# Expert 0's input from one-hot products, three expert lists from one-hot rows, held weights, and a pool of their own for the last block's rows

## The chip, the cores and the metric

The kernel runs on one core of a Trainium2 chip. TensorE (PE) multiplies, VectorE (DVE) and ScalarE (ACT) do elementwise work, GpSimd (POOL) issues the indirect transfers, SyncE (SP) issues the plain ones. The metric is the device time of one execution in microseconds. A kernel is timed several times and the median is quoted.

## The reference

Three stages, all in fp32: attention within hash buckets, an MLP with silu, and a top-1 choice of 8 experts with a skip gate.

```python
def _moe_ref(x, w_in, w_out):                 # x 1536 x 512, w_in 512 x 2048
    h = x @ w_in
    g = h * (1.0 / (1.0 + np.exp(-h)))
    return (g @ w_out).astype(np.float32)
def _moe2_ref(x, w_skip, w_gate, w1, w2):     # w1 8 x 512 x 1024, w2 8 x 1024 x 512
    do_compute = x @ w_skip > 0
    out = x.copy()
    xc = x[do_compute]
    logits = xc @ w_gate
    e_idx = np.argmax(logits, axis=1)
...
    for e in range(E):
        mask = e_idx == e
        h = np.maximum(xc[mask] @ w1[e], 0.0)
        y[mask] = gate_w[mask, None] * (h @ w2[e])
    out[do_compute] = xc + y
```

`gate_w` is the softmax probability of the chosen expert. A token with a skip score of zero or less keeps its row x.

## The kernel before

The span has three parts. Attention runs to about 237 us. Then come the MLP items: three blocks of 512 tokens, 16 slices of the 2048 hidden columns each. An item is 12 hidden matmuls (`ph`, L608) and 12 output matmuls (`o`, L642 and L651), because every fp32 number is split into a high and a low part and three products are added. The last part routes the tokens and runs the eight experts.

Weights arrive in pieces of 512 KB (`wraw`, issued by `fill`). ScalarE casts the high part `whi` (L249), VectorE subtracts to get the low part `wlo` (L252). Each expert uses eight such pieces. There are only a few places ("homes") for split pieces; `ahead()` splits the next piece whenever a matmul group has given its home back.

Routing works by block. Logits of blocks 0 and 1 are made on VectorE beside the MLP items, four at a time (`logit`, L664). `route` then finds each token's expert, its rank among the tokens of that expert (matmuls with a triangle and with ones) and its slot in a list. For experts 0 and 1 a one-hot matrix `oh` (L745) times token numbers gives the list at once (L752, L767). All lists are also written to DRAM by four GpSimd scatters a block (`id_d`, L780).

The last block's route stands in the way of the experts. Its MLP output is transposed (`xt`, L946), its logits are made by matmul (`pl`, L949), turned (`plc`, L960) and routed; the rows go to `x_d` in DRAM. Expert 0's rows are then fetched by an indirect transfer through `eid` (`xg`, L672, `fetch_x`), transposed (`tr`, L1027) and split (`xTh` L1020, `xTl` L1021); only then its first matmul (`eh`, L1049) can run. `em_busy` (L973) issues matmuls whose result nobody reads, while TensorE has nothing else to do.

Lists of experts 2 to 7 are read back from DRAM (`eidr`, L1001), transposed and cast (L1126) after expert 1's first hidden product. Gate values go to DRAM (`g_d`) and are fetched by list (`ggc`, `fetch_g`). At an expert's end VectorE makes `eo` (L1079), gate times output plus row, and GpSimd scatters it (L1010).

What runs when is written by hand. `plan` is a list of steps: ("h", e, c, j) is a quarter of expert e's hidden products, ("y", e, j) a quarter of its output products, ("t", e, c) the transposes of a hidden half (`hT0`, `hT1`), ("x", e) the transposes of the fetched rows. Each engine runs its instructions in the order in which the program issues them.

Of the kernel before, what the change touches and what calls it, by code (L numbers as in the profile page):

```python
# [9 lines left out]
F32 = mybir.dt.float32  # L10
# [9 lines left out]
P = 128  # L20
BIG = 2.0 ** 40
NB = 6


@with_exitstack
def kernel(
# [68 lines left out]
    list1 = cp.tile([P, 1], F32, name="list1")  # L95
# [494 lines left out]
    ggc = sm.tile([P, NE, 2], F32, name="ggc", bufs=1)  # L590
# [79 lines left out]
    def gathered(ix, src, cols, tag, xg=None):  # L670
        xg = pools["e"].tile([P, cols], F32, tag=tag, name=tag, bufs=4) if xg is None else xg
        nc.gpsimd.indirect_dma_start(  # L672
            out=xg, out_offset=None, in_=src, in_offset=bass.IndirectOffsetOnAxis(ap=ix, axis=0),
            bounds_check=NTOK, oob_is_err=False)
        return xg
# [4 lines left out]
    def fetch_g(e):  # L680
        ggs[e] = gathered(eid[:, e:e + 1], g_d, 1, "gg", ggc[:, e, 0:1])


    def route(t0, t1, Lx, ps, idx, ps0=None):

        n = t1 - t0
        last = t1 == NT
        if t0 == 0:
            nc.tensor.matmul(idx, c_one, c_dum, start=True, stop=False)
        Lt, st, cm = Lx[:, :, 0:NE], sel[:, t0:t1], cmp_[:, t0:t1]  # L690
        pr = ps[:, 0:n * NE].rearrange("p (t e) -> p t e", e=NE)
        pr0 = ps0[:, 0:n].unsqueeze(2) if last else pr[:, :, 0:1]

        def base(pr, w):

            nc.tensor.matmul(pr, c_one, pre[:, t0, 0:w].unsqueeze(1).to_broadcast([P, n, w]), start=True, stop=False)

        def ranks(pr, st, w):

            for t in range(n - 1):  # L700
                nc.tensor.matmul(pr[:, t + 1:n], c_one, st[:, t:t + 1].to_broadcast([P, n - 1 - t, w]), start=False, stop=False)
            nc.tensor.matmul(pr, c_u, st, start=False, stop=True)

        if last:
            base(pr0, 1)
        base(pr, NE)
        mx = sm.tile([P, n], F32, tag="mx", name="rmx")
        nc.vector.tensor_reduce(mx, Lt, axis=AX.X, op=ALU.max)
        nc.vector.tensor_scalar(cm, Lx[:, :, NE], 0.0, None, op0=ALU.is_gt)
        eq = sm.tile([P, n, NE], F32, tag="eq", name="eq")  # L710
        em = c_em.unsqueeze(1).to_broadcast([P, n, NE])
        nc.vector.tensor_tensor(eq, Lt, mx.unsqueeze(2).to_broadcast([P, n, NE]), op=ALU.is_equal)
        if last:

            st0 = sm.tile([P, n, 1], BF16, name="st0", bufs=1)
            nc.vector.tensor_tensor(st0, eq[:, :, 0:1], cm.unsqueeze(2), op=ALU.mult)
            ranks(pr0, st0, 1)
            yield
        else:
            st0 = st[:, :, 0:1]  # L720

        def choice():
            nc.vector.tensor_tensor(eq, eq, em, op=ALU.mult)
            ix = sm.tile([P, n], F32, tag="ix", name="ix")
            nc.vector.tensor_reduce(ix, eq, axis=AX.X, op=ALU.min)
            yield
            nc.vector.tensor_tensor(eq, em, ix.unsqueeze(2).to_broadcast([P, n, NE]), op=ALU.is_equal)
            nc.vector.tensor_tensor(st, eq, cm.unsqueeze(2).to_broadcast([P, n, NE]), op=ALU.mult)
            yield

        ch = choice()
        next(ch)
        if not last:
            next(ch)
            yield
            ranks(pr, st, NE)
            yield

        sl = sm.tile([P, n, NE], F32, tag="sl", name="sl")

        def onehot(e, pr, st):
            key = sm.tile([P, n], F32, tag="key", name="key")
            nc.vector.scalar_tensor_tensor(key.unsqueeze(2), pr, 1.0, st, op0=ALU.add, op1=ALU.mult)
            oh = sm.tile([P, 5, P], BF16, tag=f"oh{e}", name="oh", bufs=1)
            nc.vector.tensor_tensor(oh[:, 0:n], c_iota.unsqueeze(1).to_broadcast([P, n, P]),  # L745
                                    key.unsqueeze(2).to_broadcast([P, n, P]), op=ALU.is_equal)
            return oh

        oh0 = onehot(0, pr0, st0)
        yield  # L750
        for j in range(n):
            nc.tensor.matmul(idx, oh0[:, j], c_tok[:, t0 + j], start=False, stop=(last and j == n - 1))  # L752
        if last:
            with nc.allow_low_precision(reason="integers below 2048, exact"):
                nc.vector.tensor_reduce(eid[:, 0:1], idx, axis=AX.X, op=ALU.add)
            fetch_x(0)
            yield
            next(ch)
            ranks(pr, st, NE)
            yield  # L760
        nc.vector.tensor_tensor(sl, pr, c_e0.unsqueeze(1).to_broadcast([P, n, NE]), op=ALU.add)
        oh1 = onehot(1, pr[:, :, 1:2], st[:, :, 1:2])
        nc.vector.tensor_tensor(sl, sl, st, op=ALU.mult)
        yield
        idx1 = ps[:, 480:483]
        for j in range(n):
            nc.tensor.matmul(idx1, oh1[:, j], c_tok[:, t0 + j], start=(j == 0), stop=(j == n - 1))  # L767
# [3 lines left out]
        if last:  # L771
            fetch_x(1)
# [57 lines left out]
    with tc.manual_schedule():  # L830
# [135 lines left out]
        for g in sp:  # L966
            next(g)
# [265 lines left out]
```

## Time and profile before

| | us |
|---|---|
| median of 3 runs | 618.39 (617.16 to 620.01) |
| the profiled execution | 618.0 |
| its span, first to last instruction | 616.2 |
| end of the last block's output matmuls | 494.96 |
| first matmul of expert 0 | 508.88 |
| first matmul of expert 2 | 533.66 |

The granted TensorE clock is 0.997 of full speed in the mean, so no stage runs at the lower clock. The profile's times count from the span's first instruction. A row of the timeline gives start, duration, engine, line, operation, tiles, and in square brackets the idle time before it on its engine with what released it. From expert 2 on each expert takes 12.3 us of TensorE.

### The profile page before, as it was taken

Reading aid. Unit: us, or ns where it says so; the run is one execution under the profiler, and the core shown is the slowest. Engines: PE = TensorE matmul, PEld = TensorE weight load, DVE = VectorE, ACT = ScalarE, POOL = GpSimd, SP = SyncE. Lnnn points to the kernel's source line nnn. Section 1 sums busy time; section 2 is a strip of 40 time slices with the busy share of each in tenths; the row PEclk is TensorE's granted clock in tenths of the full one; section 3 lists DMA queues with packets and bytes.
Section 4 is the critical chain, followed back from the end, with each engine's and each line's share of the span. In section 5 each row is a group of like instructions: output and inputs, shape, how many; then the busy total and the mean of one; then the engine's idle time right before and its main releaser. Section 6 shows DMA issues by size and latency. Waiting matters only on the chain.

```text
span 616.2 us, 9579 instructions
## 1 busy us (share of the span) xinstructions
PE 598.2 (97%) x3263; PEld 462.5 (75%) x3263; DVE 465.2 (75%) x861; ACT 400.9 (65%) x671; POOL 170.1 (28%) x256
## 2 busy tenths in 40 slices
PE   7999999999999999999999999999999978999996
PEld 5767667676766767788888888888888856888885
DVE  7877778888787667799847775457784559899992
ACT  7988888888877985466554433444333456888881
POOL 6545637383654143000000000020000055633101
PEclk9999999999999999999999999999999999999998
DMA  5434542524324131666423000034223358999900
GB/s 157 124 122 104 157 124 65 151 67 138 81 65 120 49 116 49 219 208 225 154 101 115 1 1 1 1 80 154 82 96 102 136 156 242 374 407 407 404 34 28
DMA packets 30978, 83.47 MB, mean 135 GB/s; under 512 B 6032, under 2 KB 9810, under 8 KB 30798
## 3 DMA queue, kind: packets, MB, share of 16 engines
q1 hardware_dynamic: 28834, 79.06, 38.9%
q0 software_dynamic: 1936, 3.65, 1.8%
q8 instruction: 26, 0.43, 0.3%
q14 instruction: 26, 0.21, 0.1%
q10 hardware_dynamic: 156, 0.11, 0.1%
HBM read 67.66 MB, written 8.50 MB: 124 GB/s over the span
## 4 chain that ended last, share of the span: by engine, by line
PE 86%; DMA 3%; DVE 3%; ACT 3%; issue 2%; POOL 1%; SPq 0%; POOLq 0%; DVEq 0%; ACTq 0%
PE ph L608 20%; PE o L651 13%; PE S L385 11%; PE T L411 10%; PE pv L425 10%; PE o L642 7%; PE eh L1049 6%; PE ey L1071 6%; ACT P L399 1%; PE tr L1027 1%; DVE wlo L252 1%; PE pj L337 1%; DMA xg<-x_d,eid 1%; DMA w<-in_mw_dram 1%; DMA raw<-in_qT_dram 1%
## 5 line engine op out<-in xcount | busy, mean ns | idle before, releaser
L252 DVE TENSOR_TENSOR wlo<-wraw,whi 128x1024 fp32r<-128x1024 f32 x100 | 119.5, 1221 | 5.0 <-ACT whi L249 3.5
L249 ACT CAST whi<-wraw 128x1024 fp32r<-128x1024 f32 x100 | 102.8, 1051 | 21.3 <-DVE wraw L223 14.6
L399 ACT ACTIVATE P<-S,bs 128x768 f32<-128x768 f32 x96 | 95.4, 994 | 25.7 <-DVE bs L397 24.0
L614 ACT ACTIVATE g<-ph 128x512 f32<-128x512 f32 x48 | 28.7, 597 | 115.3 <-PE ph L608 112.0
L395 DVE TENSOR_REDUCE mx<-S 128x1 f32<-128x768 f32 x96 | 91.1, 949 | 10.9 <-PE S L385 8.6
L385 PE MATMUL S<-K,Q 88*128 88x384 f32 (+1 forms) x384 | 91.9, 360 | 3.6 <-ACT P L399 3.0
L411 PEld LDWEIGHTS T<-ident,P 128*128 128x128 f32 x576 | 67.9, 140 | 30.9 <-ACT PT L414 22.1
L411 PE MATMUL T<-ident,P 128*128 128x128 f32 x576 | 88.6, 277 | 0.2 <-ACT PT L414 0.2
L616 DVE TENSOR_TENSOR gl<-g,gh 128x512 fp32r<-128x512 f32 x48 | 33.6, 699 | 66.0 <-ACT gh L615 66.0
L780 POOL DMA_INDIRECT id_d<-tk,slot x12 | 12.4, 1036 | 244.7 <-DVE pre L788 241.6
L425 PE MATMUL pv<-PT,v 128*64 128x384 f32 x384 | 72.3, 498 | 0.0
L385 PEld LDWEIGHTS S<-K,Q 88*128 88x128 f32 (+1 forms) x384 | 62.4, 190 | 11.8 <-ACT P L399 5.8
L416 DVE COPY PT<-T 128x384 f32<-128x384 f32 x85 | 47.0, 553 | 22.5 <-PE T L411 22.4
L414 ACT COPY PT<-T 128x384 f32<-128x384 f32 x107 | 50.5, 479 | 7.2 <-PE T L411 6.9
L608 PE MATMUL ph<-xhi,wlo 128*128 128x512 f32 x192 | 51.5, 390 | 0.9 <-DVE wlo L252 0.9
L608 PE MATMUL ph<-xhi,whi 128*128 128x512 f32 x192 | 52.3, 394 | 0.0
L608 PE MATMUL ph<-xlo,whi 128*128 128x512 f32 x192 | 51.4, 389 | 0.0
L325 POOL TENSOR_TENSOR K<-raw,K 64x192 fp32r<-64x192 f32 x56 | 31.6, 595 | 51.5 <-ACT K L317 34.6
L664 DVE CUSTOM_DVE_ANT_0 junk<-x,gwb 128x512 bf16<-128x512 f32 x72 | 45.4, 687 | 0.0
L330 POOL TENSOR_TENSOR Q<-raw,Q 64x192 fp32r<-64x192 f32 x64 | 36.9, 605 | 28.2 <-ACT Q L320 26.5
L425 PEld LDWEIGHTS pv<-PT,v 128*64 128x64 f32 x384 | 23.4, 136 | 25.7 <-issue 25.6
L608 PEld LDWEIGHTS ph<-xhi,wlo 128*128 128x128 f32 x192 | 36.0, 188 | 8.8 <-DVE wlo L252 1.3
(173 smaller groups left out, 1042.6 us busy)
## 6 DMA issues: line engine op xcount, KB each, us to landing
wraw<-in_w_dram SPq DMA_DIRECT2D x64, 512.0 KB
w<-in_mw_dram SPq DMA_DIRECT2D x32, 512.0 KB
v<-in_vt_dram SPq DMA_DIRECT2D x8, 384.0 KB
rb<-r_d SPq DMA_DIRECT2D x32, 96.0 KB
out_dram<-x SPq DMA_DIRECT2D x12, 256.0 KB
x_d<-x SPq DMA_DIRECT2D x11, 256.0 KB
raw<-in_kT_dram SPq DMA_DIRECT2D x7, 384.0 KB
raw<-in_qT_dram SPq DMA_DIRECT2D x7, 384.0 KB
```

Of the source, the lines that this page charges most:

```text
L249: nc.scalar.copy(hi[:, sl], t[:, sl])
L252: eng.tensor_tensor(lo[:, sl], t[:, sl], hi[:, sl].bitcast(F32), op=ALU.subtract)
L385: nc.tensor.matmul(ps[:, c, 0:HQ], q_[0:n, hd, q0:q0 + P], k_[0:n, hd, c * HQ:(c + 1) * HQ], start=first, stop=not first)
L395: nc.vector.tensor_reduce(mx[:, 0:1], ps[:, :, 0:HQ], axis=AX.XY, op=ALU.max, negate=True)
L399: nc.scalar.activation(pt.rearrange("p (a b) -> p a b", a=2), ps[:, :, 0:HQ], AF.Exp, bias=bs_[:, 0:1], scale=bs_[:, 1:2], accum_out=st_su ...
L411: nc.tensor.transpose(ps[:, j], pt[:, k * P:(k + 1) * P], ident)
L414: nc.scalar.copy(dst, ps)
L416: nc.vector.tensor_copy(dst, ps)
L425: nc.tensor.matmul(st_pv[u][hd * D:(hd + 1) * D], vts[i][:, k, hd], st_PT[u][:, hd, k], start=(k == 0), stop=(k == KT - 1))
L608: nc.tensor.matmul(p_[:, 0:c1 - c0], w[:, k * P:(k + 1) * P], x[:, k, t0 * P + c0:t0 * P + c1], start=(q == 0), stop=(q == len(ops3) - 1))
L651: nc.tensor.matmul(acc[t], g[:, (t - t0) * P:(t - t0 + 1) * P], w[:, DM:PIECE], start=(f == 0 and q == 0), stop=(f == NF - 1 and q == 2))
L664: nc.vector.tensor_tensor_reduce(junk, xts[t], pools["gwb_t"][:, c], op0=ALU.mult, op1=ALU.add, scale=1.0, scalar=0.0, accum_out=L[:, t, c ...
```

## The change

- Lists of three experts, not two, are built from one-hot rows in blocks 0 and 1 (`lists`, `NL`), and five logits instead of four are made an item. After block 1, `route` fetches expert 0's rows of blocks 0 and 1 from `x_d` (rows not listed point at a row of zeros), and three items later transposes them to `xT0p`.
- In the last block the logits go ahead of the 16 transposes, the table of the exponential is loaded earlier, and `picked` multiplies the block's rows (`late`) by an fp32 one-hot matrix `ohf`: 16 products give the block's part of expert 0's transposed input. `summed` adds `xT0p`, `parted` makes the low part. No gather stands before expert 0's matmuls; its rows are still fetched, later, for `eo`.
- The third list, the slots, the scatters of the last block, the gates and the list read-back are now steps that run after given entries of `plan` (`between`). The lists of experts 3 to 7 are turned and cast after ("y", 1, 0) instead of ("h", 1, 0, 0); the read-back is issued by GpSimd, the gate write by ScalarE's queue.
- Weights are held: during expert 0 only pieces 3 to 7 are split, one at a time, and `ahead()` starts again after ("t", 0, 1). The last block's x tiles have a pool of their own (`m_lx`).

```diff
+        n = t1 - t0
         plx = ps_tile("pl", [P, 512], "X")
...
+        def turned(t):
+            for k in range(KD):
+                nc.tensor.transpose(xps[t][:, k], xt[k][:, t * P:(t + 1) * P], ident)
+            x = lxp.tile([P, DM], F32, tag="x", name="x", bufs=n)
+            nc.scalar.copy(x, xps[t].rearrange("p k c -> p (k c)"))
+            nc.sync.dma_start(x_d[(t0 + t) * P:(t0 + t + 1) * P], x)
             late.append(x)
...
+        def picked(k):
+
+            for t in range(n):
+                nc.tensor.matmul(xT0[k // 2][:, k % 2], late[t][:, k * P:(k + 1) * P], ohf[:, t], start=(t == 0), stop=(t == n - 1))
...
+        def summed(j):
+            nc.vector.tensor_tensor(xs0[:, 2 * j:2 * j + 2], xT0[j], xs0[:, 2 * j:2 * j + 2], op=ALU.add)
+            nc.scalar.copy(xTs0[0][:, 2 * j:2 * j + 2], xs0[:, 2 * j:2 * j + 2])
...
-        xTs[0] = parts(xgs[0], "xT", 2)
-        next(sp[0], None)
-        next(sp[1], None)
-        next(sp[2], None)
-        next(sp[3], None)
-        nc.vector.tensor_copy(mxc, mxf)
+        xTs[0] = tuple(xTs0)
+
+        def third_list():
+
+            ps = psE.tile([P, KD, P], F32, tag="T", name="li", bufs=3)
+            listed(ps[:, 0, 0:3], ohs[2], t0, t1)
+            added(eid[:, 2:3], ps[:, 0, 0:3], 2)
+            fetch_x(2)
+            fill(3, True)
+            nc.vector.tensor_tensor(sl, sl, st, op=ALU.mult)
+            slots(t0, t1, sl)
+            fetch_x(0)
+            fill(3, True)
+            next(sp[1], None)
+            next(gt, None)
+
+        def gates_out():
+
+            gp = psE.tile([P, KD, P], F32, tag="T", name="gp", bufs=3)
+            nc.tensor.transpose(gp[0:NT, 0], gat, ident)
+            gT = sm.tile([NT, P], F32, name="gT", bufs=1)
+            nc.scalar.copy(gT, gp[0:NT, 0])
+            nc.scalar.dma_start(g_d[0:NTOK].rearrange("(t p) c -> t (p c)", p=P), gT)
+            fetch_g(0)
+            fetch_g(1)
+            nc.gpsimd.dma_start(eidr, id_d.rearrange("(e r) c -> e (r c)", e=NE)[NL:NE, 0:P])
+            fill(1, True)
+            for t, x in enumerate(late):
+                nc.sync.dma_start(out[(t0 + t) * P:(t0 + t + 1) * P], x)
+            cnt["hold"] = 0
+
+        def other_lists():
+
+            ps = psE.tile([P, KD, P], F32, tag="T", name="eT", bufs=3)
+            nc.tensor.transpose(ps[:, 0, 0:NE - NL], eidr, ident[0:NE - NL, 0:NE - NL])
+            nc.vector.tensor_copy(eid[:, NL:NE], ps[:, 0, 0:NE - NL])
+            fetch_x(3)
+            fetch_g(2)
...
+        def one_ahead():
+
+            next(sp[3], None)
+            split(cnt["spl"])
+
+        between = {("h", 0, 0, 0): third_list, ("h", 0, 0, 1): lambda: next(sp[2], None), ("h", 0, 1, 1): gates_out,
+                   ("t", 0, 0): one_ahead, ("y", 1, 0): other_lists, ("h", 3, 0, 0): lambda: counts(t0, t1), ("y", 3, 0): largest}
...
-            if n + 1 == len(plan) or plan[n + 1][0] not in "tx":
+            between.get((what, e, *at), int)()
+            if (e or (what, *at) == ("t", 1)) and (n + 1 == len(plan) or plan[n + 1][0] not in "tx"):
                 ahead()
```

GpSimd's order, from the last block's routing to the fetch of expert 3's rows, before. `id_d` are the scatters of a block's slots, `xg` the gathers of an expert's rows, `ggc` of its gates, `wraw` a cell written ahead of a weight load.

```order
L780 DMA id_d<-tk,slot 12288x1 x8
L672 DMA xg<-x_d,eid 128x512
L181 MEMSET wraw 1x1 x3
L672 DMA xg<-x_d,eid 128x512
L780 DMA id_d<-tk,slot 12288x1 x4
L181 MEMSET wraw 1x1 x3
L672 DMA ggc<-g_d,eid 128x1 x2
L181 MEMSET wraw 1x1
L672 DMA xg<-x_d,eid 128x512
L672 DMA ggc<-g_d,eid 128x1
L672 DMA xg<-x_d,eid 128x512
L1010 DMA out_dram<-eo,eid 1536x512
```

The same place now; `xg_5216` is the early gather of expert 0's rows of blocks 0 and 1.

```order
L674 DMA xg_5216<-x_d,eidp 128x512
L742 DMA id_d<-tk,slot 12288x1 x4
L674 DMA xg<-x_d,eid 128x512 x2
L182 MEMSET wraw 1x1 x3
L742 DMA id_d<-tk,slot 12288x1 x4
L674 DMA xg<-x_d,eid 128x512
L182 MEMSET wraw 1x1 x3
L674 DMA ggc<-g_d,eid 128x1 x2
L1157 DMA eidr<-id_d 5x128
L182 MEMSET wraw 1x1
L1054 DMA out_dram<-eo,eid 1536x512
L674 DMA xg<-x_d,eid 128x512
```

The rows of experts 1 and 2 are now fetched first, expert 0's only after the scatters, and the first gate gather is the eighth indirect transfer from the block's routing on; expert 3's rows come after the scatter of expert 0's output.

VectorE's order, before, from expert 0's `xTl` to that of expert 2:

```order
L1021 TENSOR_TENSOR xTl<-tr,xTh 128x256 x2
L252 TENSOR_TENSOR wlo<-wraw,whi 128x1024 x4
L1093 CAST mxc<-mxf 128x1
L252 TENSOR_TENSOR wlo<-wraw,whi 128x1024 x2
L1021 TENSOR_TENSOR hT0l<-tr,hT0h 128x512
L252 TENSOR_TENSOR wlo<-wraw,whi 128x1024 x3
L1021 TENSOR_TENSOR xTl<-tr,xTh 128x512
L1021 TENSOR_TENSOR hT1l<-tr,hT1h 128x512
L252 TENSOR_TENSOR wlo<-wraw,whi 128x1024
L1126 CAST eid<-eT 128x6
L252 TENSOR_TENSOR wlo<-wraw,whi 128x1024 x3
L1079 SCALAR_TENSOR_TENSOR eo<-ey,ggc,xg 128x512
```

And now, from the gates (`gat`, behind the second of the held pieces) to expert 2's `xTl`:

```order
L918 TENSOR_REDUCE gat<-gex 128x12
L919 TENSOR_SCALAR gat<-gat 128x12
L920 RECIPROCAL gat<-gat 128x12
L253 TENSOR_TENSOR wlo<-wraw,whi 128x1024
L1065 TENSOR_TENSOR hT0l<-tr,hT0h 128x512
L253 TENSOR_TENSOR wlo<-wraw,whi 128x1024 x2
L1065 TENSOR_TENSOR xTl<-tr,xTh 128x512
L1065 TENSOR_TENSOR hT1l<-tr,hT1h 128x512
L253 TENSOR_TENSOR wlo<-wraw,whi 128x1024 x7
L1123 SCALAR_TENSOR_TENSOR eo<-ey,ggc,xg 128x512
L1065 TENSOR_TENSOR hT0l<-tr,hT0h 128x512
L253 TENSOR_TENSOR wlo<-wraw,whi 128x1024 x4
```

Behind the last row stand the cast of `eid`, one more `wlo`, and expert 2's `xTl`; two `wlo` and the third list's steps stand ahead of the first. The number of `wlo` up to that tile is 17 in both; three of them have moved behind expert 1's `xTl`, and gates, third list and slots stand among them.

## Rows read from the trace of the kernel before

**Rows 1.** The page: busy us (share of span), instructions, by engine.
```profile
PE 598.2 (97%) x3263; PEld 462.5 (75%) x3263; DVE 465.2 (75%) x861; ACT 400.9 (65%) x671; POOL 170.1 (28%) x256
```

**Rows 2.** The chain of waits: start us, us, what, line.
```profile
494.96 1.75 PE xt L946 x16
496.70 1.57 PE pl L949 x32
502.29 5.64 DMA xg<-x_d,eid
509.69 2.04 DVE wlo L252 x2
...
533.66 3.02 PE eh L1049 x12
```

**Rows 3.** Timeline, 496 to 511: start, us, engine, line, operation.
```profile
498.30 0.29 DVE L960 COPY plc<-pl 128x128 f32<-128x128 f32 x1 [0.71 <-PE pl L949]
...
500.18 0.69 DVE L745 TENSOR_TENSOR oh<-ct,key 128x512 bf16<-128x512 f32 x1
...
500.93 0.25 PE L752 MATMUL idx<-cb,oh 128*128 128x3 bf16 x4 [0.44 <-DVE oh L745]
...
505.25 0.20 DVE L918 RECIPROCAL gat<-gat 128x8 f32<-128x8 f32 x1
505.32 1.02 POOL L780 DMA_INDIRECT id_d<-tk,slot  x1 [0.30 <-DVE gat L916]
...
507.51 0.32 SPq L993 DMA_DIRECT2D g_d<-gT  x1
...
508.88 0.50 PE L1049 MATMUL eh<-whi,xTh 128*128 128x512 f32 x1 [0.24 <-ACT xTh L1020]
508.93 0.76 DVE L1021 TENSOR_TENSOR xTl<-tr,xTh 128x256 fp32r<-128x256 f32 x2 [2.07 <-ACT xTh L1020]
```

**Rows 4.** Busy us by stage: PE, PEld, DVE, ACT, POOL; clock, DMA share, GB/s.
```profile
509.60:533.70 24.10, 22.42 (x109) 17.65 (x107) 22.85 (x25) 17.83 (x23) 15.43 (x12) 1.00 0.88 283
...
546.20:599.50 53.30, 53.30 (x259) 44.29 (x259) 51.30 (x55) 45.80 (x57) 11.53 (x10) 1.00 0.78 308
```

**Rows 5.** Timelines of GpSimd, VectorE and TensorE, 511 to 541.
```profile
515.43 2.05 POOL L672 DMA_INDIRECT ggc<-g_d,eid  x1 [5.11 <-DMA g_d<-gT]
517.79 3.66 POOL L672 DMA_INDIRECT ggc<-g_d,eid  x1 [0.30 <-issue]
...
523.43 1.95 POOL L672 DMA_INDIRECT xg<-x_d,eid  x1 [1.90 <-DVE eid L1126]
...
527.94 1.00 POOL L672 DMA_INDIRECT xg<-x_d,eid  x1 [0.30 <-issue]
...
523.00 0.16 DVE L1126 CAST eid<-eT 128x6 int32<-128x6 f32 x1
...
525.53 2.36 DVE L252 TENSOR_TENSOR wlo<-wraw,whi 128x1024 fp32r<-128x1024 f32 x2 [1.03 <-ACT whi L249]
527.81 0.74 DVE L1079 SCALAR_TENSOR_TENSOR eo<-ey,ggc,xg 128x512 f32<-128x512 f32 x1
...
533.70 0.68 DVE L1021 TENSOR_TENSOR xTl<-tr,xTh 128x512 fp32r<-128x512 f32 x1
...
539.24 0.60 PE L1027 MATMUL tr<-ident,xg 128*128 128x128 f32 x4
```

**Rows 6.** DMA issues, 490 to 617: issues, median us to landing.
```profile
id_d<-tk,slot POOLq DMA_INDIRECT x8, 4.3
xg<-x_d,eid POOLq DMA_INDIRECT x8, 7.2
ggc<-g_d,eid POOLq DMA_INDIRECT x8, 5.4
```

**Rows 7.** Groups by line and shape, 475 to 545: busy us, mean ns.
```profile
L955 ACT COPY x<-xt 128x512 f32<-128x512 f32 x1 | 0.6, 587 | 0.1
```

More of the change, by code (lines that the diff above doesn't have):

```diff
@@ L680, in fetch_g @@
     def fetch_g(e):
-        ggs[e] = gathered(eid[:, e:e + 1], g_d, 1, "gg", ggc[:, e, 0:1])
-    def route(t0, t1, Lx, ps, idx, ps0=None):
-        n = t1 - t0
[L687 to L708, printed above, removed]
+        ggs[e] = gathered(eid[:, e:e + 1], g_d, 1, ggc[:, e, 0:1])
@@ L722, in choice @@
[L722 to L737, printed above, removed]
@@ L749, in route @@
[L749 to L761, printed above, removed]
@@ L762, in route @@
[L762 to L767, printed above, removed]
-        p1 = sm.tile([P, 1], F32, tag="p1", name="p1")
-        nc.vector.tensor_reduce(p1, idx1, axis=AX.X, op=ALU.add)
-        nc.vector.tensor_tensor(eid[:, 1:2] if last else list1, p1, list1, op=ALU.add)
-        if last:
-            fetch_x(1)
@@ L776, in route, with listed, added, slots @@
+    def listed(dst, oh, t0, t1):
+        for j in range(t1 - t0):
+            nc.tensor.matmul(dst, oh[:, j], c_tok[:, t0 + j], start=(j == 0), stop=(j == t1 - t0 - 1))
+    def added(dst, ps, e):
+        p1 = sm.tile([P, 1], F32, tag="p1", name="p1")
+        nc.vector.tensor_reduce(p1, ps, axis=AX.X, op=ALU.add)
+        nc.vector.tensor_tensor(dst, p1, lists[:, e:e + 1], op=ALU.add)
+    def slots(t0, t1, sl):
+        sf = sm.tile([P, t1 - t0], F32, tag="sf", name="sf")
         nc.vector.tensor_reduce(sf, sl, axis=AX.X, op=ALU.add)
@@ new lines @@
+        em_busy(2)
+        ohb = sm.tile([P, 5, P], BF16, tag="oh0", name="oh", bufs=1)
+        nc.scalar.copy(ohb[:, 0:n], ohf)
+        next(sp[0])
+        choice(t0, t1, pl, mxl)
+        nc.vector.tensor_copy(L[:, t0:t1], pl)
+        gt = gates(0, NT)
+        next(gt)
+        st = sel[:, t0:t1]
+        picked(0)
+        picked(1)
+        ranks(pr, st, n, NE)
+        summed(0)
+        next(sp[1])
+        sl = sm.tile([P, n, NE], F32, tag="sl", name="sl")
+        nc.vector.tensor_tensor(sl, pr, c_e0.unsqueeze(1).to_broadcast([P, n, NE]), op=ALU.add)
@@ new lines @@
+        keys = [keyed(pr[:, :, e:e + 1], st[:, :, e:e + 1], n) for e in (1, 2)]
+        ohs = [ohb] + [sm.tile([P, 5, P], BF16, tag=f"oh{e}", name="oh", bufs=1) for e in (1, 2)]
+        onehot(ohs[1][:, 0:n], keys[0], n)
+        picked(2)
+        picked(3)
+        parted(0)
+        onehot(ohs[2][:, 0:n], keys[1], n)
+        for e in (0, 1):
+            listed(ps[:, 464 + 16 * e:467 + 16 * e], ohs[e], t0, t1)
+        summed(1)
+        next(sp[2])
+        next(sp[3])
+        added(eid[:, 1:2], ps[:, 480:483], 1)
@@ L1003 @@
+        fetch_x(1)
+        added(eid[:, 0:1], ps[:, 464:467], 0)
+        parted(1)
+        next(sp[0], None)
+        eidr = sm.tile([NE - NL, P], F32, name="eidr", bufs=1)
         psR_st.close()
         pools["psL_st"].close()
-        xo_st.close()
         psE, psE_st = opened("e_ps", 2, PSUM)
```

219 lines of the change are left out of this document (123 added, 96 removed).

## The prediction

> **What bounds the kernel now.** I read the page's busy shares first. TensorE is busy 97% of the span and VectorE 75% [rows 1], so as an average TensorE is the bound; the change, however, lies in the last fifth, and averages say nothing of a stretch. So next comes the chain of waits [rows 2]. Up to 496.7 every piece is TensorE's. Then 12 us go by in which TensorE only fills in time: the logits of the last block, the routing, and a gather of 5.64 us (`xg<-x_d,eid`) that ends at 507.93. What the reader should see below it is that the chain then passes to VectorE (`wlo`, L252) and returns to TensorE: expert 0's first matmul starts at 508.88 and expert 2's at 533.66 [rows 2, 3].
>
> The table by stage says why [rows 4]. From 509.60, the start of the first held remainder `wlo`, to 533.70, the start of expert 2's `xTl`, VectorE is busy 22.85 of 24.10 us; TensorE is busy 22.42. Both queues are nearly full there. From 546.20 to 599.50 TensorE is busy 53.30 of 53.30 and nothing is to be had. So whatever is gained ahead of expert 0 lasts only if VectorE's queue up to `xTl` of expert 2 moves forward as well.
>
> **The change, part by part.** All times are on the clock of the profiled run before: 618.0 us, of which 616.2 us are the span; it lies 0.4 us under the median of 618.39, and I add differences to the median.
>
> *A. MLP stage.* Added on TensorE: four transposes of expert 0's early rows (L789 of the new kernel) and a third group of list products for blocks 0 and 1. Sixteen transposes took 1.75 us [rows 2], so four take 0.44. A group of four list products is 0.25 us of busy time [rows 3], of which some is overlap; taken at 0.11 each, 0.22 for two. Sum +0.66, all on the path, since TensorE is never idle there; bounds 0.4 to 0.9. The early gather and five logit products an item instead of four run on other engines beside matmuls: zero. Were that cover gone, each would delay one item by under a microsecond.
>
> *B. The way to expert 0.* The 16 transposes (1.75 us, [rows 2]) go behind the logits, so `plc`, at 498.30 [rows 3], comes at 496.55. From `plc` to the end of the one-hot `oh` it took 500.87 - 498.30 = 2.57; the new chain has the same kinds of steps (reduce, compare, rank, key, one-hot) and ends about 499.1. The four x copies, 0.59 each on ScalarE [rows 7], stand behind the table load, now earlier, and behind transposes that are spread between routing matmuls; I put their last end at 499.9 (bounds 499.1, when the one-hot is ready, and 500.9). A transposed-input product in fp32 isn't in the trace. The nearest row is L949: 16 products of the program show as 32 records [rows 2], two each, and a 128x128 record is 0.11 us in the transposes (1.75/16). So 0.22 each; bounds 0.11, one record, and 0.44, twice the records. Thirteen of the sixteen can only run once the last copy is there: 2.8 us. Ranks and two list groups stand between, 0.25 and 2 x 0.17. First expert matmul: 499.9 + 2.8 + 0.6 = about 503.4, against 508.88: **5.5 us earlier**. The gather of 5.64, its transposes and the wait for them leave the path.
>
> VectorE comes later to its first remainder than TensorE to its first matmul. From 499.1 it owes nine small steps (0.16 to 0.20 each, [rows 3, 5]; 1.6), then waits for the eighth product, about 501.0; then half a sum (0.38, half of `xTl` in two pieces, 0.76, [rows 3]), three small steps 0.5, two one-hots at 0.69 [rows 3], half a remainder 0.38, half a sum 0.38, four small steps 0.7, half a remainder 0.38: 4.1 us, so 505.2 against 509.60, **4.4 us earlier**.
>
> *C. VectorE's queue becomes the bound.* Between its first held remainder and `xTl` of expert 2 the order shows 17 `wlo` before and 17 after. Holding weights back only puts three of them behind expert 1's tile instead of in front (nine ahead of that tile before, six now). The helpers that used to run while TensorE waited now stand inside: six for the third list and the slots, three for the gates, 9 x 0.18 = 1.6, less 0.15 for `mxc`. So 505.2 + 22.85 + 1.6 - 0.15 + the 1.25 idle kept = 530.75, against 533.70: of 5.5 us **2.95 are left** (the idle gone or doubled: 4.2 or 1.7). On the way TensorE loses the rest: the relu ahead of expert 1's second half now stands behind six weight casts of ScalarE instead of two, and at expert 2 it waits for `xTl`.
>
> *D. Expert 0's gate values.* `eo` of expert 0 (527.81, [rows 5]) reads gathered gates, and everything VectorE has queued stands behind it. Its turn comes at about 523.7: 505.2, the 18.2 us that lay between, 1.6 of helpers, less the 1.03 idle that fell there and 0.3 of steps gone. On GpSimd the gate gather now is eighth: behind the gathers of experts 1, 2 and 0, and four scatters. At 1.3 us apiece (a scatter's 1.02 and the 0.30 ahead of it, [rows 3]) from 505.4 it starts about 515.2; where a gather overlaps a `wlo` it takes 2.05, once 3.66, instead of 1.0 [rows 5], which gives 518.3. It also waits for the gate write: before, issued at 507.51 and used at 515.43, 7.9 us later [rows 3, 5]; other small writes landed in 4.3 [rows 6]. The write now leaves ScalarE about 511.0, so 515.3 to 518.9. Landing 5.4 later [rows 6], or 7.0: 520.7 to 525.9. Stall 0 to 2.2; I take 1.0, nearest to the busy queue's rows.
>
> *E. Expert 3's rows.* The list of experts 3 to 7 is turned and cast after expert 1's first output product, not its first hidden product; the cast stands in VectorE's queue one remainder ahead of `xTl` of expert 2, 529.5 + 1.0 = 530.5, where it was at 523.00 [rows 5]. The gather follows 0.4 us later and needs 7.2 in the median [rows 6]: 538.1, or 539.2 if its issue falls in a remainder (1.95 against 1.00, [rows 5]). TensorE asks for it at 539.24 - 2.95 + 1.0 = 537.3. Stall 0 (landing in 5.64, as the first gather) to 2.3; I take 1.3. Before, the gather started at 527.94 and had 11 us.
>
> Held weight loads, late output writes and counts moved back lie beside the full queues; the weights that are used then were loaded long before. From 546.20 on the pace is TensorE's [rows 4] and keeps whatever shift there is.
>
> Sum: +0.65 - 2.95 + 1.0 + 1.3 = 0.0. **Forecast 618.4 us.**
>
> **Rivals.**
> *The small transfers are in time.* If gates land by 523.7 and expert 3's rows within 6.4 us of issue (the first gather took 5.64, [rows 2]), D and E are zero: 618.39 + 0.65 - 2.95 = 616.1. Against it: the median of eight gathers is 7.2 [rows 6], in a stretch where weights fill the queues. [...]
>
> *The front's gain stays.* If VectorE absorbs the helpers in its gaps and remainders aren't awaited, TensorE keeps 5.5: 618.39 + 0.65 - 5.5 = 613.5. For it: 1.25 us of idle. Against it: 22.85 busy of 24.10 [rows 4].
>
> *Slower: gates late.* The place is `eo` of expert 0 on VectorE. Each microsecond that the gates land after 523.7 holds all later remainders, and `eo` has no cover. With E at 1.3 the time is 617.4 plus that stall; from a landing at 527.8 on it is over 0.5% slower. With the write at 518.9, an issue of 3.66 instead of 2.05 and a landing of 7.2, it is 528: 621.9. For it: each of these has occurred in [rows 5, 6]; against: not all together.
>
> *Slower: products cost double* (0.44): 13 x 0.22 = 2.9 more, first matmul at 506.3, VectorE as late: 621.3. Against it: the two records in [rows 2]. Here the change does not do what it says, since product and gather would cost about the same.
>
> **How the numbers follow.** Forecast 0.48; transfers in time 0.20; front's gain kept 0.08; gates late 0.16; products double 0.08. A measurement here can tell about 0.5%, 3.1 us, from no change: 615.3 and 621.5. Faster: 0.08, and 0.06 from the low tails of the first two cases, 0.14. Slower: 0.10 of the gates, 0.03 of the products, 0.02 of the forecast's tail, 0.15. Same: 0.71. The range leaves out the kept front (0.08) and about 0.1 above: 615.0 to 622.0.
>
> **What would show it.** Step A: four transposes and `plc` about 497.2. B: first expert matmul near 504 and no gather ahead of it; 506 or more would speak for double products. C: `xTl` of expert 2 on VectorE near 531 to 533, TensorE waiting for it; if TensorE is without idle there, C is wrong. D: `eo` of expert 0 waiting for `ggc`, or starting with no idle ahead. E: TensorE at expert 3's transposes waiting for `xg`. If VectorE's steps from 501.0 to 505.2 cost more than the 4.1 of B, all of C shifts with them, and the forecast is too low.

## The result and the profile after

The changed kernel takes 622.68 us in the median (621.40 to 623.46), against 618.38 for the kernel before on the same chip: ratio 1.0066, 95% interval 1.0037 to 1.0095. On another chip, called the second chip below, with more executions, the ratio was 1.0041 (1.0024 to 1.0059). By these two ratios the change costs 2.5 to 4 us where no change was forecast, and the time lies outside the range of 615.0 to 622.0. The profiled execution took 623.46 us, its span is 621.3.

The chain of waits in the profile after, from the last output matmuls to expert 3 (start us, us, what), to be read beside [rows 2]:

```profile
490.11 2.72 PE o L643 x12
493.27 2.77 PE o L643 x12
496.04 1.10 PE pl L951 x32
...
499.97 1.89 PE xT L1000 x16
501.96 1.88 PE xT L1000 x16
504.01 1.48 PE eh L1093 x6
505.62 1.23 POOL xg L674
510.06 4.59 DMA wraw<-in_w_dram
514.65 5.79 ACT whi L250 x6
...
534.85 7.32 DMA xg<-x_d,eid
542.30 1.36 PE tr L1071 x8
543.66 6.79 PE eh L1093 x24
```

The gather of expert 0's rows is gone from the chain. In its place two groups of products (`xT`) of 1.9 us each stand ahead of expert 0. But the chain now ends in a gather all the same: that of expert 3's rows, 7.32 us, and behind it hidden products that take 6.79 us. Before, they took 5.46:

```profile
540.27 5.46 PE eh L1049 x24
```

The table counts from the end of the last block's output matmuls (493.27 + 2.77 = 496.04 after, 494.96 before), so that a start some tenths earlier or later does not matter. It gives the time at which TensorE starts a step.

| us from the end of the output matmuls | before | after | difference |
|---|---|---|---|
| first matmul of expert 0 | 13.92 | 7.84 | -6.1 |
| transposes of expert 1's rows | 24.21 | 17.00 | -7.2 |
| of expert 2's rows | 37.43 | 34.91 | -2.5 |
| of expert 3's rows | 44.28 | 46.26 | +2.0 |
| of expert 4's rows | 56.54 | 60.18 | +3.6 |
| end of the span | 121.26 | 125.31 | +4.1 |

The MLP stage itself, from its first matmul to that end, is 1.0 us longer (269.17 to 270.18). With the +4.1 this is the 5.1 us between the two spans. So the front gave more than forecast, but 9.2 us went again between expert 1's and expert 3's rows, 1.7 in expert 3 and 0.4 behind it.

Of the 9.2 us, 6.5 are more waiting (the four waits in the rows further down are 7.0, against 0.5 before) and 1.7 are TensorE's clock. From 505.31 to 533.51 the granted clock was 0.94 in the mean (seventh number, behind the busy times):

```profile
505.31:533.51 28.20, 24.50 (x113) 18.99 (x112) 24.07 (x34) 19.47 (x27) 14.79 (x18) 0.94 0.71 227
```

By shorter stretches it was 1.00 up to 529.3, 0.50 from 529.3 to 532.7, behind a wait of 2.57 us, and 1.00 from there to 542.3. At 0.50 the work of 1.7 us takes 3.4. In the kernel before, the clock was 0.50 only from 612.7 on, when TensorE had no work left.

The waits of TensorE from 510 to 560 after (timeline, rows of TensorE with idle ahead of them, in brackets with what ended it):

```profile
520.98 0.66 PE L1071 MATMUL tr<-ident,hr 128*128 128x128 f32 x4 [0.89 <-ACT hr L1098]
527.90 0.73 PE L1115 MATMUL ey<-whi,hT0l 128*128 128x512 f32 x2 [2.57 <-DVE hT0l L1065]
534.25 0.74 PE L1093 MATMUL eh<-whi,xTl 128*128 128x512 f32 x2 [0.36 <-DVE xTl L1065]
542.30 0.66 PE L1071 MATMUL tr<-ident,xg 128*128 128x128 f32 x4 [3.18 <-DMA xg<-x_d,eid]
```

VectorE there, to be read beside [rows 5]:

```profile
505.31 1.22 DVE L253 TENSOR_TENSOR wlo<-wraw,whi 128x1024 fp32r<-128x1024 f32 x1
...
515.73 8.04 DVE L253 TENSOR_TENSOR wlo<-wraw,whi 128x1024 fp32r<-128x1024 f32 x7
526.50 0.75 DVE L1123 SCALAR_TENSOR_TENSOR eo<-ey,ggc,xg 128x512 f32<-128x512 f32 x1 [2.73 <-issue]
...
532.30 0.16 DVE L1167 CAST eid<-eT 128x5 int32<-128x5 f32 x1
...
533.51 0.69 DVE L1065 TENSOR_TENSOR xTl<-tr,xTh 128x512 fp32r<-128x512 f32 x1
```

`eo` of expert 0 has its turn at 515.73 + 8.04 = 523.77 and starts at 526.50. The row names no releaser; on the second chip the same row reads `[2.33 <-DMA ggc<-g_d,eid]`. TensorE's 2.57 us for `hT0l` is the shadow of this wait, since `hT0l` stands behind `eo`.

GpSimd after:

```profile
515.83 2.05 POOL L674 DMA_INDIRECT xg<-x_d,eid  x1 [0.30 <-issue]
...
521.37 1.01 POOL L674 DMA_INDIRECT ggc<-g_d,eid  x1 [3.34 <-DMA g_d<-gT]
522.69 1.95 POOL L674 DMA_INDIRECT ggc<-g_d,eid  x1 [0.30 <-DVE wlo L253]
524.64 0.59 POOL L1157 DMA_DIRECT2D eidr<-id_d  x1
525.20 0.09 POOL L182 MEMSET wraw<- 1x1 f32 x1
533.03 1.52 POOL L1054 DMA_INDIRECT out_dram<-eo,eid  x1 [7.75 <-DVE eid L1167]
534.85 1.98 POOL L674 DMA_INDIRECT xg<-x_d,eid  x1 [0.30 <-DVE hT1l L1065]
```

These rows run one behind the other: GpSimd stood idle for 7.75 us ahead of the scatter, and the gather of expert 3's rows started 0.30 us behind it. The memset at 525.20 stands behind the gate gathers. SyncE's next weight load waits for this memset, and in SyncE's order the writes of the last block's output stand behind that load:

```profile
525.69 2.37 SPq L1160 DMA_DIRECT2D out_dram<-x  x4
```

Before, these four writes went out at 511.64. The scatter of expert 0's output goes to the same tensor and waits for them. `eo` was ready at 527.25; the scatter starts at 533.03, and the gather of expert 3's rows stands behind it. The profile names the cast of `eid` as releaser of the scatter, the last event on VectorE; the program's order has the scatter wait for the four writes. That this is so was a theory at this point, and the experiments test it. The landings bear it out: the last of the four writes landed at 532.20, and the scatter started 0.83 us later; on the second chip the scatter started at 532.50, when the cast (532.37 to 532.52) was not yet done.

### The profile page after: what moved, and what is told of

It is laid out like the page before. It is cut to its first block, busy times and chain, and to the rows that moved or that the text cites. A ratio compares the mean times of both kernels' runs of the same rounds, so it can differ in the third digit from the quotient of the medians.

```text
span 621.3 us, 9605 instructions
## 1 busy us (share of the span) xinstructions
PE 601.3 (97%) x3274; PEld 465.5 (75%) x3274; DVE 468.5 (75%) x875; ACT 402.6 (65%) x674; POOL 171.3 (28%) x258
## 4 chain that ended last, share of the span: by engine, by line
PE 83%; DMA 5%; ACT 4%; DVE 3%; issue 2%; POOL 1%; SPq 1%; POOLq 0%; DVEq 0%; ACTq 0%
PE ph L609 20%; PE o L652 13%; PE S L386 10%; PE T L412 10%; PE pv L426 10%; PE o L643 7%; PE eh L1093 5%; PE ey L1115 4%; ACT P L400 2%; PE tr L1071 1%; DMA xg<-x_d,eid 1%; DVE wlo L253 1%; ACT whi L250 1%; PE pj L338 1%; DMA wraw<-in_w_dram 1%
## 5 line engine op out<-in xcount | busy, mean ns | idle before, releaser
L742 POOL DMA_INDIRECT id_d<-tk,slot x12 | 14.3, 1190 | 148.1 <-DVE pre L752 144.9
L331 POOL TENSOR_TENSOR Q<-raw,Q 64x192 fp32r<-64x192 f32 x64 | 36.1, 594 | 28.2 <-ACT Q L321 26.5
```

## The experiments

Each group of kernels was timed beside the kernel before on its own chip, and ratios are to that.

**Two waits by themselves.** First the output writes earlier:

```diff
             fetch_x(2)
             fill(3, True)
+            for t, x in enumerate(late):
+                nc.sync.dma_start(out[(t0 + t) * P:(t0 + t + 1) * P], x)
...
-            for t, x in enumerate(late):
-                nc.sync.dma_start(out[(t0 + t) * P:(t0 + t + 1) * P], x)
             cnt["hold"] = 0
```

> Changed kernel with one edit: the last block's four output writes are issued between the two groups of weight loads of the third-list step, no longer behind the read-back and its memset on GpSimd. Theory A (the scatter of expert 0's output waits for these writes, and the gather of expert 3's rows stands behind that scatter on GpSimd): the gather starts at about 532.9 instead of 534.85, right after the cast of the lists, rows land near 540.1, TensorE waits 1.2 us instead of 3.2 there and does not fall to the lower clock behind it (1.3 us): 619.4 us, or 620.7 if the clock still falls. Rival B (VectorE's queue alone costs the time, as forecast in term C): nothing changes, 622.7. Rival C (rows come late because the transfer queues are full, whenever issued): the gather starts earlier but lands at 542 all the same, 622.7.

Measured: 622.05 us, ratio 1.0019 (0.9999 to 1.0040). The writes went out at 511.44, and the scatter started as soon as `eo` was done (529.75, scatter at 530.03). But the gates came later still:

```profile
518.63 1.92 POOL L674 DMA_INDIRECT ggc<-g_d,eid  x1 [0.17 <-issue]
...
529.00 0.75 DVE L1123 SCALAR_TENSOR_TENSOR eo<-ey,ggc,xg 128x512 f32<-128x512 f32 x1 [4.79 <-DMA ggc<-g_d,eid]
```

The gather that started at 518.63 was awaited until 529.00, 10.4 us, so the cast behind it slipped to 534.80 and the gather of rows to 535.23. TensorE did not wait for rows any more, but 4.7 us for `hT0l`. Theory A is right in the wait that went and wrong in the start it forecast. Its 619.4 us was reckoned on the first chip and is a ratio of 1.0017, so the number came out (with an interval that ends next to the changed kernel's 1.0041), but not by the way that was forecast: TensorE itself came late to the rows, since its clock was 0.50 from 530.1 to 536.9 with the wait of 4.7 us, and expert 3 then ran at 1.00. That the 1 MB of writes, moved forward, delayed the gates fits a second kernel with early writes below, whose `eo` waited for the gates too: from the gate gather's start to `eo` it was 10.4 us here and 11.1 there, and 5.1 to 8.3 in five profiles of the changed kernel and its variants with late writes in which `eo` waited.

Then the gates' wait alone. This kernel leaves expert 0's gates out of its output:

```diff
-nc.vector.scalar_tensor_tensor(o[:, c0:c1], py, ggs[e], xgs[e][:, c0:c1], op0=ALU.mult, op1=ALU.add)
+nc.vector.scalar_tensor_tensor(o[:, c0:c1], py, cmp_[:, 0:1] if e == 0 else ggs[e], xgs[e][:, c0:c1], op0=ALU.mult, op1=ALU.add)
```

> Changed kernel, but expert 0's output is multiplied by a value that has long been in memory instead of its gathered gate; the gather still runs. This leaves the gate of expert 0 out, and with it the wait of 2.7 us ahead of eo of expert 0. Theory A: the wait goes, TensorE's 2.6 us at expert 1's second output half go too, but the time does not, since the late output writes still hold the scatter, and with it the gather of expert 3's rows, until about 532.9: TensorE waits about 5.8 us there instead of 3.2; total 622.7, within 0.7. Rival (the two stalls add up, as the prediction summed them): 620.1.

Measured: 622.82 us, ratio 1.0048 (1.0026 to 1.0070), as the changed kernel with 1.0041 and 1.0066. The time alone does not decide: on the first chip the expected 622.7 is a ratio of 1.0070, the rival's 620.1 one of 1.0028, and both lie in the interval. The profile does. `eo` started at 523.52 without idle, yet in the count of the table the span ends at 125.18, against 125.31 and 125.43 in the changed kernel's two profiles. The chain of this run shows why nothing came of it:

```profile
524.76 6.54 DMA out_dram<-x
...
532.14 0.39 POOL out_dram L1054
...
534.35 6.77 DMA xg<-x_d,eid
541.16 1.97 PE tr L1071 x8
543.13 7.06 PE eh L1093 x24
```

The last of the late writes is in flight from 524.76 to 531.30. Behind it come the scatter and the gather of expert 3's rows, and TensorE waits 5.0 us for them. So the late writes are on the chain, and the two stalls do not add up: with the gates' wait gone, the other takes its place.

**The order of the scatter and the gather.**

```diff
                 if j == 3:
...
+                    if e == 0:
+                        held_o.append(o)
-                    if len(cuts) == 1:
+                    elif len(cuts) == 1:
...
             fetch_x(3)
+            scatter(eid[:, 0:1], held_o[0], out)
             fetch_g(2)
```

> Changed kernel with one edit: the scatter of expert 0's output is issued on GpSimd behind the gather of expert 3's rows. Theory A: the gather starts right behind the cast, at about 532.8 instead of 534.85; the rows land 2 us earlier, TensorE waits 1.2 instead of 3.2 us and the clock falls less: 2 to 3 us under the changed kernel, ratio 1.002 to 1.004 to the kernel before. Rival C (rows land late whenever issued): same as the changed kernel, 1.0066.

With it ran the changed kernel again:

> The changed kernel itself, beside the runs of the kernel before that the other kernels of this group share, since single edits move the time by less than the chip's own spread. All theories: a ratio of 1.005 to 1.008 to the kernel before, and the same places in the trace: eo of expert 0 idle 2 to 3 us for the gates, TensorE idle about 3 us for expert 3's rows, and the lower clock for some of the time behind it.

Measured on one chip: changed kernel 622.41 us, ratio 1.0041 (1.0024 to 1.0059); scatter behind the gather 620.56 us, 1.0011 (0.9997 to 1.0025). The edit is worth about 1.9 us. Expert 3's rows came 2.2 us earlier in the count of the table (44.13 against 46.37), and TensorE's wait for them fell from 3.73 to 0.49:

```profile
534.56 1.80 POOL L674 DMA_INDIRECT xg<-x_d,eid  x1 [9.68 <-DVE eid L1170]
536.65 1.03 POOL L1054 DMA_INDIRECT out_dram<-eo,eid  x1 [0.30 <-issue]
```

Both kernels still waited for the gates, 2.3 and 2.7 us at `eo`. With TensorE's share of that wait, 2.55 us, the clock was 0.50 from 529.3 to 536.1 in the edited kernel, which delayed expert 2; expert 3 took 12.4 us instead of 13.9.

The other way round, the writes late in the kernel before, where the rows' gather stands ahead of the scatter:

```diff
+        fill(1, True)
         for t, x in enumerate(late):
             nc.sync.dma_start(out[(t0 + t) * P:(t0 + t + 1) * P], x)
-        fill(1, True)
         cnt["hold"] = 0
```

> The kernel before with one edit: the last block's four output writes are issued one weight load later, behind the memset on GpSimd that follows the gate gathers, near 521.6 instead of 511.6, as in the changed kernel. There the gather of expert 3's rows stands ahead of the scatter of expert 0's output. Theory A: the scatter waits a little (writes landing near 529), but no row is late: ratio 1.000 within 0.002. Rival C (late output writes cost time by themselves, in the full queues): ratio 1.003 or more.

Measured: 619.24 us, ratio 0.9996 (0.9976 to 1.0016). The scatter waited until 532.83, and no row was late. So late writes by themselves show no cost here (the interval leaves room for 1 us); what counts is what stands behind the scatter.

**Gates early, and all three.** In the first try the gates' last steps, transpose and write went into the step of the third list:

```diff
             fetch_x(2)
+            next(gt, None)
+            gp = psE.tile([P, KD, P], F32, tag="T", name="gp", bufs=3)
+            nc.tensor.transpose(gp[0:NT, 0], gat, ident)
...
+            nc.scalar.dma_start(g_d[0:NTOK].rearrange("(t p) c -> t (p c)", p=P), gT)
             fill(3, True)
```

> Changed kernel with the gates' last three VectorE steps, their transpose and the write to DRAM moved into the third-list step, ahead of the slots and scatters; the gathers of the gates stay where they are. The write is then issued near 507.5 instead of 511.14, before the first scatter. Theory A2 (the write of the gates lands late because it goes out among the four scatters, about 5 us behind the last of them): it lands well before 517, the gate gather starts at about 518 as soon as GpSimd is free, and eo of expert 0 has no wait or under 0.7 us. Rival (this write takes 8 to 10 us anyway): it lands at 516 to 517.5, and the gather's start does not tell; the landing does. For the total theory A expects 621.5 to 622.7, since the read-back, the memset behind it and the late output writes move up by about 3 us as well: the writes land near 530, the cast at about 529.7 and the gather of expert 3's rows at about 531: then TensorE's wait there stays about 3 us, and the time is 619.5 to 620. A time of 622.7 would speak against the place of the late writes on the chain.

Measured: 620.53 us, ratio 0.9997 (0.9979 to 1.0015). `eo` had no wait, as theory A2 has it, and the ratio is under all that was expected (619.5 us is 1.0018 on the first chip). TensorE, however, stood 2.21 us at the transpose, since the gates' steps came behind a remainder on VectorE, and behind that wait its clock was 0.50 from 508.9 to 512.3 (128x512 matmuls start every 0.43 us there, 0.23 before it), which takes 1.7 us more: expert 1 began 3.8 us later than in the changed kernel. The scatter still started at 530.22, behind the late writes. Adding the early writes and the cast on ScalarE (`nc.scalar.copy(eid[:, NL:NE], ps[:, 0, 0:NE - NL])`) gave

> Changed kernel with three edits: output writes early, gate write early, and the cast of the lists of experts 3 to 7 on ScalarE instead of VectorE, so that it does not stand behind four remainders. Theory A: gather of expert 3's rows at about 529.3, rows at 536.5, no wait of more than 0.5 us at expert 3, no wait ahead of eo of expert 0, no lower clock; what stays is VectorE's queue up to expert 2's tile (term C): 618.4 - 2.7 + 0.4 = 615.5 to 616.5. Rival B (VectorE's queue alone is what costs): at most 1 us under the changed kernel. Rival C (transfers land late whenever issued): about 620.

Measured: 619.38 us, ratio 0.9984 (0.9962 to 1.0006), a miss. The wait at the transpose stayed (2.21), and with it a clock of 0.50 (up to 510.7, again a matmul every 0.43 us); the gather of rows started at 530.39 but took 4.64 us to issue on GpSimd, among remainders, and TensorE waited 0.80 us for its rows.

Second try: the gates' three steps on VectorE ahead of the first held remainder, transpose and write a hidden quarter later, the cast on ScalarE, and either early writes or the scatter behind the gather.

```diff
         parted(1)
+        next(gt, None)
         next(sp[0], None)
...
-        between = {("h", 0, 0, 0): third_list, ("h", 0, 0, 1): lambda: next(sp[2], None), ("h", 0, 1, 1): gates_out,
+        def gates_early():
...
+        between = {("h", 0, 0, 0): third_list, ("h", 0, 0, 1): gates_early, ("h", 0, 1, 1): gates_out,
```

With early writes:

> Changed kernel with three edits: the gates' last steps on VectorE ahead of the first held remainder, their transpose and write one hidden quarter later (so that TensorE does not wait for them, as it did for 2.2 us in the run with all three edits), the cast of the lists on ScalarE, output writes of the last block between the two weight groups. Theory A (three waits on GpSimd's queue cost the time; what stays is VectorE's queue): expert 1's first matmul back at 514.3, xTl of expert 2 at 531 to 532, no wait over 1 us at expert 3, no lower clock; 2 to 3 us under the kernel before: ratio 0.995 to 0.997. Rival B (VectorE's queue or the transfers take the gain anyway): ratio 1.000 or above.

Measured: 619.30 us, ratio 0.9997 (0.9979 to 1.0014), a miss. `eo` waited 3.27 us for the gates again, as with early writes alone, and the clock was 0.50 from 527.5 to 534.4.

With the scatter behind the gather:

> As the kernel with gates, cast and output writes, but the output writes stay where the changed kernel has them, and the scatter of expert 0's output is issued on GpSimd behind the gather of expert 3's rows instead of ahead of it. Theory A: the place of the scatter, not the writes themselves, was the cost; rows of expert 3 are fetched near 529, ratio 0.995 to 0.997, about as with early writes. Rival C (the writes themselves, 1 MB in the full queues, hold the rows): expert 3's rows land 2 us later than with early writes, ratio about 1.000.

Measured: 617.07 us, **ratio 0.9953 (0.9934 to 0.9971)**, 2.9 us under the kernel before by this ratio, 2.5 by the medians, and so faster than both. GpSimd in this run:

```profile
517.20 1.92 POOL L674 DMA_INDIRECT ggc<-g_d,eid  x1 [0.17 <-issue]
519.42 1.95 POOL L674 DMA_INDIRECT ggc<-g_d,eid  x1 [0.30 <-issue]
521.38 0.59 POOL L1155 DMA_DIRECT2D eidr<-id_d  x1
521.93 0.09 POOL L182 MEMSET wraw<- 1x1 f32 x1
528.35 1.80 POOL L674 DMA_INDIRECT xg<-x_d,eid  x1 [6.33 <-ACT eid L1165]
531.54 1.98 POOL L1055 DMA_INDIRECT out_dram<-eo,eid  x1 [1.40 <-DVE wlo L253]
```

and TensorE's remaining waits over a microsecond:

```profile
533.27 0.73 PE L1095 MATMUL eh<-whi,xTl 128*128 128x512 f32 x2 [1.49 <-DVE xTl L1066]
```

No wait for rows, a granted clock of 1.00 in every stretch from 505 to 604. What is left is VectorE: expert 2's `xTl`. In the count of the table, TensorE turns expert 3's rows at 40.62, against 44.28 before: 3.7 us ahead, less 0.9 for the longer MLP stage. This kernel has three edits at once; what the cast on ScalarE is worth by itself was not run.

That VectorE's queue is this rest was tried by splitting one more piece ahead of expert 1's tile, where VectorE was idle for 1.0 us:

```diff
             next(sp[3], None)
             split(cnt["spl"])
+            split(cnt["spl"])
```

> The kernel with early gates, cast on ScalarE and the scatter behind the gather, and one weight piece more split ahead of expert 1's tile, where VectorE was idle for 1.0 us. Term C (VectorE's queue up to expert 2's tile is the bound once the three waits are gone): expert 1's first matmul the same or 0.3 us later, xTl of expert 2 about 1.0 us earlier against the first held remainder, TensorE's wait of 1.5 us for it shrinks to about 0.5: ratio about 0.994, against 0.9953. Rival (TensorE's own work or the weights' arrival sets the pace there): no change in that wait, ratio 0.995 or above.

Measured: 617.82 us, ratio 0.9976 (0.9958 to 0.9994). TensorE's wait for `xTl` fell from 1.49 to 0.30 us as term C has it, but `eo` then stood ready a microsecond sooner and waited 2.51 us for the gates. The gain went into the next wait: TensorE stood 2.21 us at `hT0l`, and behind that its clock was 0.50 from 527.9 to 531.4. The two kernels ran on different chips, and neither time says that the one is better.

**Held weights undone.** All four held remainders at once, further pieces whenever a home is free:

```diff
         xTs[0] = tuple(xTs0)
+        for k in (1, 2, 3):
+            next(sp[k], None)
...
-            if (e or (what, *at) == ("t", 1)) and (n + 1 == len(plan) or plan[n + 1][0] not in "tx"):
+            if n + 1 == len(plan) or plan[n + 1][0] not in "tx":
```

> Changed kernel with held weights undone: all four held remainders in a row ahead of the third list, and further pieces split during expert 0 as soon as a home is free. Theory A (what counts is when GpSimd gets its lists, slots and gates, since scatters, gates, read-back and late writes follow one another there): the third list and the gates come about 3.4 us later, the gate gather at about 524, eo of expert 0 waits 4 us or more, rows of expert 3 land later by 2 to 3 us: 2 to 3 us over the changed kernel, ratio 1.009 to 1.011. Rival D (holding the weights starves TensorE or VectorE behind expert 1): ratio at or under 1.003.

Measured: 622.23 us, ratio 1.0053 (1.0029 to 1.0078): neither theory. The third list did come 3 us later (509.69 against 506.63), the gates' last step 2 (511.13 against 509.04), and expert 1 5 us later. But VectorE reached `eo` later too, at 526.77 and without idle, and rows came at 542.26, as in the changed kernel. So holding the weights shows no worth while TensorE waits for expert 3's rows, which come last either way; what it is worth in the kernel without that wait was not run.

**The clock.** In the changed kernel the granted clock falls again behind the wait for expert 3's rows, and here nothing hides it. The busy time by stage (us, busy by engine, then clock, DMA share, GB/s), first of the changed kernel's two profiles, then of the other, then of a kernel with 24 unread matmuls in the place of that wait:

```profile
538.00:542.30 4.30, 1.12 (x6) 0.58 (x5) 3.02 (x3) 0.91 (x1) 3.39 (x4) 1.00 1.04 415
542.30:551.00 8.70, 8.70 (x38) 7.29 (x39) 5.43 (x8) 6.10 (x8) 2.45 (x3) 0.80 1.02 397
```

```profile
541.00:551.00 10.00, 8.12 (x33) 6.63 (x34) 4.86 (x6) 5.54 (x7) 3.49 (x4) 0.83 1.03 397
```

```profile
541.00:551.00 10.00, 9.67 (x49) 8.13 (x50) 7.74 (x12) 8.42 (x11) 2.69 (x3) 1.00 1.03 401
```

```diff
             else:
+                if e == 3:
+                    pb = psE.tile([P, DM], F32, tag="H", name="pb", bufs=3)
+                    for _ in range(24):
+                        nc.tensor.matmul(pb[:, 0:256], c_u, cb[:, 0:256], start=True, stop=True)
                 xTs[e] = parts(xgs[e], "xT")
```

> Changed kernel with 24 matmuls of 256 columns, whose result nobody reads, ahead of expert 3's transposes (3.0 us at the 0.125 us that such a matmul takes in the routing), where TensorE waited 3.2 and 3.7 us for expert 3's rows in the two profiles. Theory A3 (part of the loss is TensorE's clock, granted at 0.80 to 0.83 of full in the 10 us behind that wait): the clock stays near 1.00 there, the hidden products of expert 3 take 5.5 us and not 6.8, and the time is about 1.3 us under the changed kernel: ratio 1.002 to 1.004 to the kernel before, against 1.0041 and 1.0066 of the changed kernel. Rival (the clock follows something else, or the slow matmuls there have another cause): granted clock as low as before, ratio 1.004 to 1.007, more if the matmuls outlast the wait.

Measured: 622.61 us, ratio 1.0054 (1.0037 to 1.0071). In the profile the expectation holds: clock 1.00, and from expert 3's transposes to expert 4's 12.3 us as before, where the changed kernel needs 13.9. In the median no gain is seen. The profiled execution was the fastest of twelve (620.91), and its gates were also a microsecond earlier than in the changed kernel's two. The earlier wait, for `hT0l`, was 1.62 us there, and the clock did not fall behind it. The kernel without held weights, above, kept 1.00 behind a wait of 3.55 us for the same rows, so the unread matmuls may not be the whole reason. Still, the fall of the clock and its 1.6 us are shown in the trace of the changed kernel; what they are worth over many executions stays open.

## Why the prediction was wrong, point by point

The forecast's times are on the clock of the run before. After, the output matmuls end 1.08 us later (496.04 against 494.96), so 1.1 us are taken off the measured times that are compared with it here.

*A, MLP stage, +0.66.* Measured +1.0, and 0.8 to 1.2 in every kernel with this stage. The four transposes are the 0.44 of the forecast. TensorE's busy time in the stage grew by no more than 0.46 (268.31 to 268.77); the rest is idle time, 0.86 before and 1.41 after, which the forecast had put at nothing. What it waits for there was not traced.

*B, the way to expert 0, 5.5 us earlier.* Right in kind, small in size: 6.1 from the end of the output matmuls. The eight products of a half took 1.89 us, 0.24 each, close to the 0.22. The rival of double products is out. VectorE's first remainder came 5.4 us earlier (505.31 - 496.04 = 9.27 against 14.64), not 4.4.

*C, VectorE's queue, 2.95 left.* Right in its length. From the first remainder to `xTl` of expert 2 are 28.2 us in the profile after, 25.5 without the 2.73 of idle at `eo`; the forecast had 25.55. In the kernel in which the three waits are gone, 3.7 us are left at expert 3, and TensorE waits for that very tile. The rival that the front's gain stays is out.

*D, gates, 0 to 2.2, taken as 1.0.* The mechanism and the place were right, the size was not: `eo` waited 2.3 to 2.7 us. Its turn came at 522.7, 1.0 us ahead of the forecast's 523.7, since VectorE's queue had started earlier, and the gates landed at 525.3, late within the bounds (520.7 to 525.9). In this profile the write was awaited 10.2 us (511.14 to 521.37) and not 7.9; on the second chip, where the transpose ahead of the write came 0.47 us later (510.61 against 510.14), the gather started at 518.67 without a wait for it, but there the gather was awaited 7.9.

*E, expert 3's rows, 0 to 2.3, taken as 1.3.* This step failed. It had the gather follow the cast by 0.4 us. In fact the gather stands behind the scatter of expert 0's output on GpSimd, and the scatter behind four output writes which the change had moved from 511.6 to 525.7. The forecast named the late writes and put them "beside the full queues"; it did not ask who waits for them. The row that shows the new order was in the order of GpSimd, where the scatter stands one place ahead of the gather; before, the gather stood ahead. The cast came at 531.2 instead of 530.5, the gather 2.55 us behind its start instead of 0.4, and the transfer took 7.32 instead of 7.2. So the landing came at 541.1, 3.0 us behind the forecast's 538.1, of which the order is 2.1, and TensorE waited 3.2 us. The kernel with only these two exchanged is 1.9 us faster, as said above. The upper end of 2.3 does not follow from the forecast's own figures either: 539.2 - 537.3 is 1.9.

*The clock* was in no term. The wait of 3.2 to 3.7 us for expert 3's rows had a second price of 1.6 us in both profiles of the changed kernel. The lower clock behind the gates' wait, in one of the two, cost nothing in the end, since TensorE then waited for the rows anyway.

*The sum.* Of the 5.1 us between the spans, 0.35 are what A lacked, 2.6 are expert 3's rows (46.26 in the table, where the forecast has 44.28 - 0.65 = 43.63), 1.7 the clock in expert 3, and 0.4 lie behind it. D and E were added, too. With the gates' wait taken away the time did not move, since the other stall took its place: the terms were two ways to the same instruction, and the later one counts. The forecast of 618.4 thus rests on a wrong E and on a sum that would not have held either. That the rival "gates late" stood at 621.9 (617.4 + 4.3 is 621.7), near what was measured, is luck: its wait occurred at 2.7 us instead of 4.3, and without this wait the kernel was no faster.

The rival "small transfers are in time" gave 616.1 on 618.39, a ratio of 0.9963. The kernel which brings them in time has 0.9953.

## What to carry to other kernels

When a step is moved, ask not only what it costs where it lands but who waits for what it writes, and what is queued behind that waiter. On GpSimd here, a scatter that waited for plain writes held the gather behind it; exchanging the two was worth 1.9 us by itself and, with gates and cast moved, made the change a gain of 0.5%. Stalls found one after another in a chain are not to be added before one of them has been taken away.

## What was not expected of the hardware

A microsecond of idle TensorE cost more than one in some places here. Around waits of 3.2, 3.7 and 5.0 us for expert 3's rows the granted clock was 0.80, 0.83 and 0.73 in the mean of stretches of 9 to 10 us (in the first of them, 0.53 from 542.8 to 546.3 and 0.99 from there to 551.0), and expert 3 took 13.9 us and more instead of 12.3. Behind a wait of 1.0 us at the same place it stayed at 1.00, and so it did behind one of 3.55 us in the kernel without held weights. Shorter waits elsewhere went with a lower clock as well: around the end of waits of 2.21, 2.55 and 2.57 us, and between two of 1.39 and 1.61 us in the kernel without held weights, it fell to 0.50, but not around waits of 1.62, 1.90 and, on the second chip, 2.19 us.

The gather of 128 gate values was awaited 5.1 us from its start in the profile after (521.37 to 526.50), 7.9 in the changed kernel on the second chip (518.67 to 526.57), and 10.4 when 1 MB of output writes went out seven microseconds ahead of it (511.44 and 518.63). The writes alone do not tell its time: in the kernel before, where they went out 3.8 us ahead of it, it landed 7.0 us from its start (515.43 to 522.46). In which queue or at which memory it is held was not traced.

An indirect transfer's issue on GpSimd took longer in many cases beside VectorE. In the profiles before and after, from 505 us on, each of the 16 issues that no remainder overlapped took 0.97 to 1.03 us. The 40 that a remainder overlapped took 0.97 to 3.66 us, 1.57 in the median, and 16 of them stayed under 1.2; in a kernel above one took 4.64. Why some are spared is open.
